# Attention and a gated MLP on one core: visits taken out of a pair's last step, differences, roundings and a weight conversion put elsewhere in their queues

## The chip, the cores and the metric

The kernel runs on one core of one Trainium2 chip. The metric is the time on the device in microseconds, the median of several runs. The engines of the core are called TensorE (PE; PEld for its weight loads), VectorE (DVE), ScalarE (ACT), GpSimd (POOL) and SyncE (SP), which here issues the transfers.

## What is computed

Eight batches of eight heads attend over 576 positions with 64 values a head. Four heads see a window of 32 positions, four see every fourth of the last 128. The result, 4608 tokens by 512, goes through a layer of 2048 with the gate h * erf(softplus(h)). The two weight matrices come as float64.

```python
scores = scale * np.matmul(q, k.transpose(0, 1, 3, 2))
...
masks = np.stack([mask_plain if h < H // 2 else mask_dil for h in range(H)], axis=0)
scores = np.where(masks[None, :, :, :], scores, -1000000000.0)
...
attn = attn / (np.sum(attn, axis=-1, keepdims=True) + 1e-09)
return np.matmul(attn, v).astype(np.float32)
...
h = x @ w_in
sp = np.maximum(h, 0.0) + np.log1p(np.exp(-np.abs(h)))
g = h * erf(sp)
return (g @ w_out).astype(np.float32)
```

## The kernel before

Every product of the MLP is made of three matmuls of rounded operands: high by high, high by low, low by high. A number is split into `hi`, its rounded value, and `lo`, the rounded remainder. `split` (L608) does that for a gate: a copy to `ghi` (L611; on VectorE, but on ScalarE for items of kind B) and a subtraction to `glo` (L612, VectorE).

**Attention** is cut into 72 units. A unit is scored in one visit (`scores`, L217, TensorE; `mask_max`, L228, eight masks for two units, VectorE), gets its exponents later (`exponents`, L238, ScalarE, with a table load ahead), is normalized (`normalize`, L249 and L250 on VectorE, L251 on GpSimd), and three visited units later it is turned (`transposes`, L256, TensorE, and the copy to `pT`, L260, VectorE) and multiplied with the values (`values`, L275, TensorE), and its rows are copied out (`rows`, L317, ScalarE). The first fourteen units are visited ahead of the MLP and seven in half steps 0 to 6, one each; later visits take two units at once. `PACE` and `visits` say where those stand: in 15 half steps from 9 to 39, and then in the periods 0 to 7 and 16 to 19.

**The MLP, first part.** Three chunks of 512 tokens are done in 24 steps of two half steps each, x = 0 to 47. A half step makes twelve products of the first matrix (L521, into the bank `h` or `tx`), takes the bank (L593), and twelve products of the second matrix (L636, into four accumulators `acc`) for the step two back, whose gate was computed in between: Softplus (L597), Erf (L600), product (L605), split. `weights` turns one more piece of the float64 weights into hi and lo (`prep_act`: L439 and L444, ScalarE; `prep_dve`: L453, L457 to L459, VectorE). At half step 11 (`SAVED`) the sums of chunk 0 are put aside: `save` copies the four accumulators (L650, two on VectorE, two on ScalarE) and stores them. The products of half step 12 that start the next sums need the accumulators empty.

**The second part** does the last six chunks in three pairs. A pair takes seven products instead of eight for four blocks (the scheme of Strassen in Winograd's form): the sums of weights are made by `build` in half steps 29 to 47 (L531, L540 to L543, L553, L557, stored to and read back from `ws`), the differences of tokens T1 to T4 by `big_less` (L716, VectorE), and each of B11, B21, B22, T1 to T4 is split by `big_hi` (L729, ScalarE) and `big_lo` (L733, VectorE). `FORE` and `AFT` list these jobs by half step and by (period, place in it).

A **period** (`period`, L837) is one step of this part. If it has a step d, it makes the seven products k = 0 to 6 (L768, six matmuls each, into `h` and `tx` in turn) and takes each from its bank on VectorE (`take_big`: L778, L776, L788). Between them stand four `quarter`s of six matmuls of the second matrix for the period's item (L636). Period i does the products of step d, Softplus for it (L801), Erf (L877) and the product (`multiply_big`, L805) for step d - 1, and the second matrix for the item i, whose first half is split a period earlier, its second at the period's start. Periods 0 to 7 are the first pair, 16 to 23 the second, 32 to 39 the third; periods 8 to 15 and so on have an item alone. In period 7 the products are grouped 3, 2, 2 and 0, so that the next Softplus starts early. The order of the products is A11 with B11, A12 with B21, S2 with T2, S3 with T3, A22 with T4, S1 with T1, S4 with B22.

All engines work strictly in the order in which the code is written, each in its own queue.

Of the kernel before, what the change touches and what calls it, by code (L numbers as in the profile page):

```python
# [41 lines left out]
NU = NIT * NBLK // PER  # L42
# [23 lines left out]
LAG = 3  # L66
# [6 lines left out]
SAVED = 2 * (HALF + 1) + 1  # L73
# [6 lines left out]
PART = 4  # L80
RIGHT = ("B11", "T3", "B21", "T2", "T1", "B22", "T4")
BUILD = 2 * SPC * 2 - 3
PACE = [9, 13, 15] + list(range(17, 40, 2))
BIG = {2 * SPC * k + d: SPC * k + d for k in range(DOUBLES) for d in range(SPC)}
ORDER = ("A11", "A12", "S2", "S3", "A22", "S1", "S4")

# [1 line left out]
def visits():  # L88


    at = {n - FIRST: [n] for n in range(FIRST, 2 * NBLK + LAG)}
    for x, n in zip(PACE, range(2 * NBLK + LAG, NU + LAG, 2)):
        at[x] = [n, n + 1]
    n, late = max(n for ns in at.values() for n in ns) + 1, {}
    for i in BIG:
        if n < NU + LAG:
            late[i] = [m for m in (n, n + 1) if m < NU + LAG]
            n += 2
    assert n >= NU + LAG
    return at, late  # L100
# [39 lines left out]
def attn_moe_kernel(ctx: ExitStack, tc: tile.TileContext, qk, v, masks, eye, w_in, w_out, out):  # L140
# [261 lines left out]
    def doubles(i):  # L402
        return io.tile([P, TOK, 2], I32, name=f"dbl{i}", bufs=1)
# [10 lines left out]
    def hold(on):  # L414
        held[0] = on
        while behind and not on:
            load, args = behind.pop(0)
            load(*args)
# [163 lines left out]
    def cell(i):  # L582
        return win[:, i * 2 * TOK:(i + 1) * 2 * TOK].rearrange("p (i n) -> p i n", i=2)
# [24 lines left out]
    def split(item, e, copy=None):  # L608
        ghi, glo = (work.tile([P, TOK], F32R, name=n) for n in ("ghi", "glo"))
        gs[item].append((ghi, glo))  # L610
        (copy or nc.vector.tensor_copy)(out=ghi, in_=e)  # L611
        nc.vector.tensor_tensor(out=glo, in0=e, in1=ghi.bitcast(F32), op=ALU.subtract)  # L612
# [28 lines left out]
    def copy_for(tt):  # L641
        return nc.scalar.copy if tt % 2 else nc.vector.tensor_copy

    def save():

        o = doubles(2).bitcast(F32).rearrange("p n w -> p (n w)")
        spare = small.tile([P, DM], F32, name="o", bufs=1)
        for tt in range(TOK // P):
            part = [o[:, 0:DM], o[:, DM:2 * DM], spare, pz[1]][tt]
            copy_for(tt)(out=part, in_=acc[tt])  # L650
            nc.sync.dma_start(out=partial[tt], in_=part)
# [7 lines left out]
    def store(c):  # L659
        last = c == NCH - 1  # L660
        for tt in range(TOK // P):
# [3 lines left out]
            else:  # L665
# [4 lines left out]
                else:  # L670
# [7 lines left out]
                    T3=(cell(6), cell(2 * len(RIGHT) + 1)), T1=xp[0:2], T4=xp[2:4]), {}  # L678
# [45 lines left out]
    def room_of(name):  # L724
        return lambda: raw[name]
# [5 lines left out]
    def big_lo(name):  # L731
        for p, r in zip(big[name], raw[name]):
# [3 lines left out]
    LESS = {n: (big_less, n, *FROM[n], room) for n, room in  # L736
            (("T3", room_w), ("T1", room_p), ("T2", room_w), ("T4", room_of("T2")))}
    HI, LO = ({n: (f, n) for n in RIGHT} for f in (big_hi, big_lo))

    FORE = {41: [(big_load, 0, ("B22",), room_w), (big_load, 0, ("B12", "B11", "B21"))],  # L740
            42: [LESS["T3"], HI["B11"]], 43: [LESS["T1"], HI["B21"]], 44: [LESS["T2"][:-1] + (room_of("B22"),)],
            45: [HI["T2"], LO["B11"]], 46: [LO["T2"]],
            47: [LESS["T4"], LO["B21"], (big_places,), (big_load, 0, ("B22",)), HI["T3"], HI["T4"], HI["T1"]]}
    AFT = {(0, 0): [LO["T3"]], (0, 1): [LO["T4"], HI["B22"]], (0, 2): [LO["T1"], LO["B22"]]}
    for k in range(1, DOUBLES):
        i = 2 * SPC * k
        first, then = (("B11", "B21"), ("B12", "B22")) if k == 1 else (("B12", "B22", "B11", "B21"), ())
        AFT.update({(i - 8, 0): [(big_load, k, first)], (i - 8, 3): [(big_load, k, then)],
                    (i - 6, 3): [LESS["T1"], LESS["T3"], HI["B11"], HI["B21"]],
# [67 lines left out]
    def split_item(item, j):  # L817
        e = ls[item] if item == NT - 2 else hs[item]
        split(item, e[:, j], nc.scalar.copy if isinstance(item, tuple) and item[0] == "B" else None)
# [17 lines left out]
    def period(i, late):  # L837
        d, item = BIG.get(i), ITEMS[i]
# [21 lines left out]
        def quarter():  # L860
            for _, args in zip(range(6), rest_):
                mm(args)

        for u in pending:
            exponents(u)
        split_item(item, 1)
        third(0)
        jobs(AFT.get((i, 0), ()))
        quarter()
# [4 lines left out]
        elif behind_ is not None:  # L874
            for kind_ in "AB":
                e = ls[kind_, behind_]
                nc.scalar.activation(out=e, in_=e, func=AF.Erf)  # L877
        jobs(AFT.get((i, 1), ()))
        quarter()
# [11 lines left out]
        if ahead is not None:  # L891
            split_item(ahead, 0)
        jobs(AFT.get((i, 2), ()))
        last_ = 6 in groups[2]
# [15 lines left out]
        if i + 3 < len(ITEMS) and isinstance(ITEMS[i + 3], tuple):  # L910
            load_g(ITEMS[i + 3])
        jobs(AFT.get((i, 3), ()))
        for n in ns:
# [10 lines left out]
    with tc.manual_schedule():  # L924
# [20 lines left out]
        def weights(x):  # L945
            if x not in pause:
                prep_act()
                prep_dve(keep=2 if SAVED - 4 < x <= SAVED else None)
# [3 lines left out]
        for x in range(2 * NT):  # L952
# [47 lines left out]
            if j == 1 and t < NT:  # L1000
                argument(t)
            if t >= 2:
                weights(x)
                mm2(t - 2, j)
                if x == SAVED:
                    save()
                    hold(False)
                    load_w(2)
                elif ends(t - 2):
                    if j == 1:  # L1010
                        store(STEPS[t - 2][0])
                    elif STEPS[t - 2][2] == 2:
                        fetch()
# [109 lines left out]
```

## Time and profile before

| | us |
|---|---|
| three runs | 905.57, 906.27, 907.35 |
| median | 906.27 |
| profiled execution, its own time | 906.74 |
| span of its trace, first to last instruction | 904.9 |
| TensorE busy | 874.4 |
| VectorE busy | 633.8 |
| ScalarE busy | 565.5 |
| GpSimd busy | 77.4 |

Busy time counts an engine's own instructions, not its waits and not the issuing of transfers. Matmuls overlap, and the profile draws each with a modelled end, so idle time on TensorE is read from the places where it says what TensorE waited for. A row of the timeline has the start, the length, the engine, the line, the operation and the tiles it writes and reads, and in brackets the idle time of the engine before it and what ended it.

### The profile page before, as it was taken

How to read it: one execution, taken by the hardware profiler on the slowest of the kernel's cores; microseconds unless marked ns; L12 is line 12 of the kernel's file. 1: busy time of each engine (PE TensorE's matmuls, PEld its weight loads, DVE VectorE, ACT ScalarE, POOL GpSimd, SP SyncE). 2: the span in 40 equal slices, each digit the busy share in tenths (PEclk: the TensorE clock that was granted, in tenths of full speed). 3: DMA queues.
4: the chain of work that ended last, by engine and by line, in shares of the span. 5: the costliest groups of instructions: out<-in, count | busy, mean ns of one | idle time of the engine just before them, and what ended most of it. 6: DMA issues, size and time to landing. Idle time of an engine off the chain costs nothing. (4 is left out here: it accounts for less than half of the span.)

```text
span 904.9 us, 20855 instructions
## 1 busy us (share of the span) xinstructions
PE 874.4 (97%) x8122; PEld 704.5 (78%) x8134; DVE 633.8 (70%) x1575; ACT 565.5 (62%) x1271; POOL 77.4 (9%) x97
## 2 busy tenths in 40 slices
PE   7799999999999999999999899899999999999998
PEld 3467878888888887788887688688888888888886
DVE  5888978987798888786776565576657647666622
ACT  6889978898788877566766552574544433535321
POOL 1212101111111100010010000000000000000000
PEclk9899999999999999999999999999999999999999
DMA  8874435464758886466665841474449225442341
GB/s 275 298 249 144 147 117 186 159 224 125 232 187 282 306 300 233 154 248 209 227 220 175 296 165 49 142 268 168 172 148 344 83 82 197 163 151 82 130 150 47
DMA packets 66915, 170.41 MB, mean 188 GB/s; under 512 B 7680, under 2 KB 14592, under 8 KB 63744
## 3 DMA queue, kind: packets, MB, share of 16 engines
q1 hardware_dynamic: 66528, 168.55, 54.1%
q8 instruction: 64, 1.05, 0.5%
q10 hardware_dynamic: 288, 0.52, 0.2%
q14 instruction: 35, 0.29, 0.1%
HBM read 122.91 MB, written 46.14 MB: 187 GB/s over the span
## 5 line engine op out<-in xcount | busy, mean ns | idle before, releaser
L636 PE MATMUL acc<-wout_hi,ghi 128*128 128x512 f32 x576 | 228.4, 397 | 5.7 <-DVE ghi L611 3.7
L636 PE MATMUL acc<-wout_lo,ghi 128*128 128x512 f32 x576 | 225.7, 392 | 0.0
L636 PE MATMUL acc<-wout_hi,glo 128*128 128x512 f32 x576 | 160.2, 392 | 0.0
L636 PEld LDWEIGHTS acc<-wout_hi,ghi 128*128 128x128 f32 x576 | 108.6, 189 | 28.3 <-DVE ghi L611 4.1
L636 PEld LDWEIGHTS acc<-wout_hi,glo 128*128 128x128 f32 x576 | 109.1, 189 | 23.3
L636 PEld LDWEIGHTS acc<-wout_lo,ghi 128*128 128x128 f32 x576 | 108.8, 189 | 21.9
L251 POOL TENSOR_TENSOR prob<-prob,rinv 128x256 f32<-128x256 f32 x72 | 70.5, 987 | 493.3 <-DVE ssum L249 269.8
L238 ACT ACTIVATE prob<-prob,nmax 128x64 f32<-128x64 f32 x288 | 96.4, 339 | 10.9 <-DVE nmax L228 10.7
L801 ACT ACT_TABLE_LOAD x24 | 30.8, 1283 | 97.4 <-DVE hc L776 49.8
L768 PE MATMUL tx<-win 128*128 128x512 f32 x288 | 74.9, 395 | 4.2 <-DVE hc L778 3.6
L228 DVE CUSTOM_DVE_ANT_0 prob<-sp,cst 128x64 f32<-128x64 f32 x288 | 45.3, 219 | 42.9 <-ACT rows L317 30.9
L768 PE MATMUL h<-win 128*128 128x512 f32 x288 | 75.2, 397 | 0.0
L768 PEld LDWEIGHTS tx<-win 128*128 128x128 f32 x288 | 53.5, 188 | 16.9 <-DVE hc L778 4.4
L768 PEld LDWEIGHTS h<-win 128*128 128x128 f32 x288 | 54.4, 191 | 12.3 <-DVE dbl L778 0.4
L612 DVE TENSOR_TENSOR glo<-hc,ghi 128x512 fp32r<-128x512 f32 x50 | 34.6, 692 | 38.3 <-PE acc L636 27.7
L238 ACT ACTIVATION_READ_ACCUMULATOR prob<-prob,nmax 128x1 f32 x288 | 54.9, 191 | 0.0
L612 DVE TENSOR_TENSOR glo<-dbl,ghi 128x512 fp32r<-128x512 f32 x48 | 33.2, 692 | 29.0 <-PE acc L636 17.5
L521 PE MATMUL h<-x,win 128*128 128x512 f32 x192 | 48.8, 396 | 0.0
L877 ACT ACTIVATE s<-s 128x1024 f32<-128x1024 f32 x48 | 48.2, 1052 | 0.3
L521 PE MATMUL tx<-x,win 128*128 128x512 f32 x192 | 48.0, 392 | 0.0
L801 ACT ACTIVATE s<-hc 128x1024 f32<-128x1024 f32 x24 | 25.5, 1061 | 35.4 <-DVE hc L776 22.9
L611 ACT CAST ghi<-hc 128x512 fp32r<-128x512 f32 x24 | 14.9, 622 | 49.1 <-PE acc L636 46.2
(146 smaller groups left out, 1518.0 us busy)
## 6 DMA issues: line engine op xcount, KB each, us to landing
win<-ws SPq DMA_DIRECT2D x24, 1024.0 KB, 5.0
v<-in_v_dram SPq DMA_DIRECT2D x72, 256.0 KB, 4.8
win<-ws SPq DMA_DIRECT2D x24, 768.0 KB, 5.1
qk<-in_qk_dram SPq DMA_DIRECT2D x48, 272.0 KB, 4.7
dbl<-in_w_in_dram SPq DMA_DIRECT2D x16, 512.0 KB, 4.4
dbl<-in_w_out_dram SPq DMA_DIRECT2D x16, 512.0 KB, 4.2
ws<-x SPq DMA_DIRECT2D x32, 256.0 KB, 3.6
qk<-in_qk_dram SPq DMA_DIRECT2D x24, 288.0 KB, 4.4
```

What stands on the lines that cost most here:

```text
L228: nc.vector.tensor_tensor_reduce(out=pr[:, g, :], in0=sps[h][:, u % 2, p, :], in1=mask[QUADS.index(kinds(u, p))], scale=-SCALE, scalar=HUG ...
L238: nc.scalar.activation(out=probs[u][:, j, :], in_=probs[u][:, j, :], func=AF.Exp, scale=-1.0, bias=nmax[:, j:j + 1], accum_out=sums[u][:, ...
L251: nc.gpsimd.tensor_tensor(probs[u], probs[u], rinv.broadcast_to([P, 2 * PARTS, KEYS]), op=ALU.mult)
L521: nc.tensor.matmul((h, bank)[j], win_at[:, ftp, j, cc // 2, w, cc % 2, :], x[cc], start=(k == 0 and i == 0), stop=(k == CC - 1 and i == 2))
L611: (copy or nc.vector.tensor_copy)(out=ghi, in_=e)
L612: nc.vector.tensor_tensor(out=glo, in0=e, in1=ghi.bitcast(F32), op=ALU.subtract)
L636: nc.tensor.matmul(args["out"], args["lhsT"], args["rhs"], start=args["start"], stop=args["stop"])
L768: nc.tensor.matmul(bank_, w[:, wi, c, :], x[c][:, xi, :], start=(c == 0 and n == 0), stop=(c == 1 and n == 2))
L801: nc.scalar.activation(out=ls[kind_, d], in_=hs[kind_, d], func=AF.Softplus)
L877: nc.scalar.activation(out=e, in_=e, func=AF.Erf)
```

## The change

Five edits in one.

1. `PACE` gets one more entry, half step 41, and `visits` gives no visit to the last step of a pair (`i + 1 in BIG`). So there is a visit at half step 41 and none in period 7. Every unit between them is visited two units earlier than before; the four visits from period 16 on stay.
2. In `FORE` the difference T4 and the remainder of B21 move from half step 47 to 46.
3. In `AFT` the remainder of T1 moves from (0, 2) to (0, 1), ahead of the product and the split that stand between the two places.
4. In `period` the split of the item's second half comes ahead of the exponents.
5. At half step 11 alone, `weights` comes behind the copies of `save`, no longer ahead of the products.

```diff
-PACE = [9, 13, 15] + list(range(17, 40, 2))
+PACE = [9, 13, 15] + list(range(17, 42, 2))
...
-        if n < NU + LAG:
+        if n < NU + LAG and i + 1 in BIG:
...
-            45: [HI["T2"], LO["B11"]], 46: [LO["T2"]],
-            47: [LESS["T4"], LO["B21"], (big_places,), (big_load, 0, ("B22",)), HI["T3"], HI["T4"], HI["T1"]]}
-    AFT = {(0, 0): [LO["T3"]], (0, 1): [LO["T4"], HI["B22"]], (0, 2): [LO["T1"], LO["B22"]]}
+            45: [HI["T2"], LO["B11"]], 46: [LO["T2"], LESS["T4"], LO["B21"]],
+            47: [(big_places,), (big_load, 0, ("B22",)), HI["T3"], HI["T4"], HI["T1"]]}
+    AFT = {(0, 0): [LO["T3"]], (0, 1): [LO["T4"], LO["T1"], HI["B22"]], (0, 2): [LO["B22"]]}
...
+        split_item(item, 1)
         for u in pending:
             exponents(u)
-        split_item(item, 1)
...
             if t >= 2:
-                weights(x)
+                if x != SAVED:
+                    weights(x)
                 mm2(t - 2, j)
                 if x == SAVED:
                     save()
+                    weights(x)
                     hold(False)
```

ScalarE's queue around the end of period 7 and in period 8, before: after the last Softplus (L801) come the visit's row copies (L317), the table load and the exponents (L238), and then Erf (L877) for the step of period 7.

```order
L801 ACTIVATE s<-hc 128x1024 x2
L317 COPY rows<-sp_90 128x112
L317 COPY rows<-sp_90 128x16
L317 COPY rows<-sp_91 128x128
L317 COPY rows<-sp_90 128x128
L317 COPY rows<-sp_91 128x128
L238 ACT_TABLE_LOAD
L238 ACTIVATE prob,ssum<-prob,nmax 128x64 x8
L877 ACT_TABLE_LOAD
L877 ACTIVATE s<-s 128x1024 x2
```

The same place now:

```order
L801 ACT_TABLE_LOAD
L801 ACTIVATE s<-hc 128x1024 x2
L877 ACT_TABLE_LOAD
L877 ACTIVATE s<-s 128x1024 x2
L611 CAST ghi<-dbl_6631 128x512
```

The rows of the visit are gone from between Softplus and Erf.

ScalarE's queue at the start of period 17, as a piece of the difference; `ghi` (L611) is the rounding of the item's second half.

```order
 L317 COPY rows<-sp_91 128x128
-L238 ACT_TABLE_LOAD
-L238 ACTIVATE prob,ssum<-prob,nmax 128x64 x8
 L611 CAST ghi<-hc 128x512
+L238 ACT_TABLE_LOAD
+L238 ACTIVATE prob,ssum<-prob,nmax 128x64 x8
 L877 ACT_TABLE_LOAD
```

The rounding now stands ahead of the table load and the exponents.

VectorE's queue in period 0, before, from taking the fourth product (`tx`) to taking the fifth (`h`) and the sixth (`tx`): `x_99` and `x_100` are the remainder of T4, `x_97` and `x_98` that of T1, `dbl_4955` and `plain` that of B22.

```order
L776 TENSOR_TENSOR dbl_4978<-tx,dbl_4978 128x512
L733 TENSOR_TENSOR x_99<-w,x_99 128x512
L733 TENSOR_TENSOR x_100<-w,x_100 128x512
L605 TENSOR_TENSOR hc<-hc,s 128x1024
L611 CAST ghi<-hc 128x512
L612 TENSOR_TENSOR glo<-hc,ghi 128x512
L733 TENSOR_TENSOR x_97<-pT_88,x_97 128x512
L733 TENSOR_TENSOR x_98<-o,x_98 128x512
L733 TENSOR_TENSOR dbl_4955<-dbl_4955 128x512
L733 TENSOR_TENSOR plain<-plain 128x512
L776 TENSOR_TENSOR dbl_4977<-h,dbl_4978 128x512
L788 TENSOR_TENSOR dbl_4978<-tx,dbl_4978 128x1024
```

The same place now:

```order
L776 TENSOR_TENSOR dbl_5088<-tx,dbl_5088 128x512
L733 TENSOR_TENSOR x_99<-w,x_99 128x512
L733 TENSOR_TENSOR x_100<-w,x_100 128x512
L733 TENSOR_TENSOR x_97<-pT_88,x_97 128x512
L733 TENSOR_TENSOR x_98<-o,x_98 128x512
L605 TENSOR_TENSOR hc<-hc,s 128x1024
L611 CAST ghi<-hc 128x512
L612 TENSOR_TENSOR glo<-hc,ghi 128x512
L733 TENSOR_TENSOR dbl_5065<-dbl_5065 128x512
L733 TENSOR_TENSOR plain<-plain 128x512
L776 TENSOR_TENSOR dbl_5087<-h,dbl_5088 128x512
L788 TENSOR_TENSOR dbl_5088<-tx,dbl_5088 128x1024
```

The remainder of T1 stands ahead of the product and the split of the item; between the fourth product and the fifth stand the same nine instructions as before.

## Prediction before the run

> **What bounds the kernel now.** I read the page first, for the busiest engine, and then the table of waits for TensorE (engine and line, what it waited for, us in total, times, longest).
>
> ```profile
> PE 874.4 (97%) x8122; PEld 704.5 (78%) x8134; DVE 633.8 (70%) x1575; ACT 565.5 (62%) x1271; POOL 77.4 (9%) x97
> ...
> PE acc L636 <- DVE ghi L611: 3.7, 1, 3.7
> PE tx L768 <- DVE hc L778: 3.6, 2, 2.6
> ...
> PE tx L768 <- DVE x L733: 2.0, 1, 2.0
> PE acc L636 <- DVE dbl L650: 2.0, 1, 2.0
> ...
> PE tx L768 <- DVE win L733: 0.6, 1, 0.6
> PE sp L275 <- DVE pT L260: 0.6, 1, 0.6
> ```
>
> TensorE is busy 97% of the span, and the change takes no matmul away. So only TensorE's idle time can be won, and time in which it runs slowly. The waits listed here make 12.5 us, seven in number, each on VectorE; they stand at half step 11, in period 0, in periods 7 and 8, and in period 17. (The second wait on L778, 0.9 us, is at the start of period 7, and the change leaves it.)
>
> The second view is the table of stretches, cut along the steps in which the granted clock changes (length, busy time of PE, PEld, DVE, ACT and POOL, then the clock, DMA share, GB/s).
>
> ```profile
> 121.71:125.12 3.41, 1.44 (x7) 1.18 (x7) 3.38 (x6) 3.36 (x5) 0.00 (x0) 1.00 0.18 69
> 125.12:128.54 3.42, 3.42 (x10) 2.63 (x9) 0.77 (x2) 1.11 (x1) 0.00 (x0) 0.50 1.04 352
> ...
> 364.06:367.47 3.41, 1.67 (x7) 1.05 (x6) 3.20 (x5) 0.00 (x0) 0.00 (x0) 1.00 0.70 276
> 367.47:370.88 3.41, 3.14 (x16) 2.61 (x17) 3.31 (x6) 0.76 (x1) 0.00 (x0) 1.00 0.00 0
> 507.42:510.83 3.41, 0.49 (x2) 0.44 (x3) 2.09 (x3) 2.01 (x3) 0.00 (x0) 1.00 0.81 287
> 510.83:514.24 3.41, 3.41 (x10) 2.64 (x9) 2.42 (x4) 0.47 (x1) 0.00 (x0) 0.50 0.38 142
> ...
> 572.27:575.68 3.41, 1.05 (x5) 0.88 (x6) 1.98 (x3) 3.38 (x8) 0.00 (x0) 1.00 0.34 125
> 575.68:579.10 3.42, 3.42 (x10) 2.64 (x9) 0.69 (x1) 0.88 (x1) 0.00 (x0) 0.50 0.02 5
> ```
>
> Three of the waits are paid twice. A stretch of 3.41 us in which TensorE was busy 1.44, 0.49 or 1.05 us is followed by one at half clock, which does 1.71 us less work. After 1.67 us busy the clock stayed whole. So in this trace the limit lies between 1.44 and 1.67 us busy, and the half clock is part of the price of the three long waits.
>
> The chain of waits gives the pace of matmuls that wait for nothing (start, us, what):
>
> ```profile
> 661.96 1.36 PE h L768 x6
> ```
>
> That is 0.227 us each. The profile draws a lone matmul 0.39 us long, so an idle stretch it shows starts 0.17 us after the next matmul could have started. Each wait therefore costs 0.17 us more than its listed length.
>
> **Half step 11: one weight conversion behind the copies.** Rows of the timeline (start, us, engine, line, operation, tiles; in brackets the idle time before and its releaser):
>
> ```profile
> 120.60 0.68 DVE L453 TENSOR_TENSOR win<-w,win 128x512 fp32r<-128x512 f32 x1
> ...
> 122.99 0.68 DVE L650 COPY dbl<-acc 128x512 f32<-128x512 f32 x1
> ...
> 123.73 0.50 PE L636 MATMUL acc<-wout_hi,ghi 128*128 128x512 f32 x1 [1.97 <-DVE dbl L650]
> ...
> 131.15 0.69 DVE L593 COPY hc<-tx 128x512 f32<-128x512 f32 x1 [5.22 <-PE tx L521]
> ```
>
> Now the copy starts where L453 started, at 120.60, and ends at 121.28; TensorE may go on 0.06 later, as it did before, at 121.34. It is ready at 123.73 - 1.97 - 0.17 = 121.59. The wait goes with 0.25 us to spare, and with it its half clock: 1.97 + 0.17 + 1.71 = **3.85 us**. What moves back is the conversion, by two copies, 1.36 us, on VectorE, and by two on ScalarE. Behind it stand the copy of h and the roundings for the next products; VectorE then sat idle 5.22 us before 131.15, and this covers 1.36 us and TensorE's earlier arrival of 3.85. Cost nothing; without that cover 1.36.
>
> **Period 0: differences and roundings moved ahead.**
>
> ```profile
> 352.30 0.69 DVE L593 COPY hc<-tx 128x512 f32<-128x512 f32 x1 [3.12 <-PE tx L521]
> ...
> 355.23 1.28 DVE L716 TENSOR_TENSOR w<-win,w 128x512 f32<-128x512 f32 x2
> 356.44 1.28 DVE L733 TENSOR_TENSOR win<-win 128x512 fp32r<-128x512 f32 x2
> ...
> 362.73 0.69 DVE L776 TENSOR_TENSOR dbl<-tx,dbl 128x512 f32<-128x512 f32 x1 [0.67 <-PE tx L768]
> ...
> 369.40 0.69 DVE L776 TENSOR_TENSOR dbl<-h,dbl 128x512 f32<-128x512 f32 x1
> ...
> 361.17 1.52 PE L768 MATMUL tx<-win 128*128 128x512 f32 x6
> ...
> 370.83 0.86 PE L768 MATMUL h<-dbl,win 128*128 128x512 f32 x3
> ```
>
> The four instructions of T4 and B21 (2.56 us) move from period 0 into half step 46, in front of the row at 352.30, where VectorE idled 3.12 us. B21's remainder is then there before the second product of period 0 asks for it: 0.60 + 0.17 = 0.77 us saved.
>
> The remainder of T1 moves in front of L605, L611 and L612, so the sixth product gets it in time, and its wait of 2.01 + 0.17 = 2.18 us goes. But VectorE still has the same work between taking the fourth product (362.73) and the fifth (369.40): 6.67 us from start to start. The seventh product writes into the bank that the fifth leaves, so it waits for that second row. Counted from the start of the fourth product: VectorE takes it 362.73 - 361.17 = 1.56 later, and the bank is free 1.56 + 6.67 + 0.69 + 0.05 = 8.97 later. TensorE arrives 370.83 - 361.17 - 2.18 = 7.48 later. **A new wait of 1.49 us stands at the seventh product**, and of 2.18 only 0.69 is kept. Sum: 0.77 + 0.69 = **1.46 us**. A wait of 1.49 leaves 1.9 of 3.41 us busy, above the 1.67 after which the clock stayed whole.
>
> **Periods 7 and 8: no visit in the last step.**
>
> ```profile
> 498.45 1.06 ACT L801 ACTIVATE s<-hc 128x1024 f32<-128x1024 f32 x1 [3.61 <-DVE hc L776]
> ...
> 506.15 1.28 ACT L877 ACT_TABLE_LOAD   x1
> 507.44 2.00 ACT L877 ACTIVATE s<-s 128x1024 f32<-128x1024 f32 x2
> ...
> 505.58 1.07 PE L636 MATMUL acc<-wout_hi,glo 128*128 128x512 f32 x4
> 510.34 0.50 PE L636 MATMUL acc<-wout_hi,ghi 128*128 128x512 f32 x1 [3.69 <-DVE ghi L611]
> ```
>
> Between the last Softplus (ends 499.51) and the table load of Erf (506.15) ScalarE copied rows and made the visit's sixteen exponents. Without the visit the load follows at once, at about 499.53. From that load to the matmul it released took 510.34 - 506.15 = 4.19 us, so ghi is there at 503.72. TensorE without waits was ready at 510.34 - 3.69 - 0.17 = 506.48; without the visit, which costs it 2.44 us (below), and without its wait for pT (0.59 + 0.17 = 0.76), at 503.28. **A wait of 0.44 us is left.** Saved: 0.76 + 3.86 + 1.71 - 0.44 = **5.89 us**.
>
> On what a change of table costs, a page speaks against this sum. The Trainium skill, "ScalarE: Activation LUTs", section "What ACT_TABLE_LOAD costs", puts every switch at about 2.66 us, 1.38 of it a drain beside the load. The trace has the Erf begin 1.29 us after its load began and shows no drain. By the page the load could not follow the Softplus so closely, the wait left would be an estimated 1.8 us and the saving 4.5.
>
> **Period 17: the split ahead of the exponents.**
>
> ```profile
> 568.68 1.28 ACT L238 ACT_TABLE_LOAD   x1 [0.17 <-DVE nmax L228]
> ...
> 572.64 0.60 ACT L611 CAST ghi<-hc 128x512 fp32r<-128x512 f32 x1
> ...
> 574.62 2.05 PE L768 MATMUL tx<-win 128*128 128x512 f32 x6 [2.65 <-DVE hc L778]
> ```
>
> The rounding on ScalarE (572.64) stood behind the exponents; behind it, on VectorE, stood the remainder and the copy that frees tx. From the rounding to the matmul took 1.98 us. Ahead of the exponents it starts by 568.68 and TensorE is released by 570.7, or by 571.3 if VectorE's masks come first. TensorE is ready at 574.62 - 2.82 = 571.80. So 2.65 + 0.17 + 1.71 = **4.53 us**. Rounding and exponents only change places, so the Erf behind them keeps its place; TensorE, 4.53 us earlier, needs its result two quarters later.
>
> **Half step 41: the visit that comes in.**
>
> ```profile
> 303.27:311.15 7.88, 7.88 (x158) 6.43 (x156) 6.76 (x14) 6.16 (x12) 2.02 (x2) 1.00 0.61 234
> 333.06:338.50 5.44, 5.44 (x25) 4.50 (x24) 5.34 (x9) 5.17 (x8) 0.00 (x0) 1.00 0.64 234
> ...
> 320.27 0.16 DVE L249 TENSOR_SCALAR ssum<-ssum 128x4 f32<-128x4 f32 x1
> ...
> 371.33 0.75 DVE L260 COPY pT<-sp 128x256 f32<-128x256 f32 x2
> ...
> L228 DVE CUSTOM_DVE_ANT_0 prob<-sp,cst 128x64 f32<-128x64 f32 x288 | 45.3, 219 | 42.9 <-ACT rows L317 30.9
> ```
>
> A half step with a visit lasts 7.88 us, one without 5.44: a visit is 2.44 us of TensorE. It leaves period 7 and enters half step 41, so it costs nothing by itself. It brings VectorE 8 masks (45.3 / 288 x 8 = 1.26 us), two copies (0.75) and four small ones (some 0.65): 2.66 us against TensorE's 2.44. ScalarE gets the rows, a table load and sixteen exponent instructions; SyncE four loads and a store, in front of the stores of the sums. VectorE was already busy 5.34 of 5.44 us in a step like 44, and half step 46 gets its 2.56 on top. So it ends half step 47 without idle time and about an us behind its old place, still in time for period 0's first roundings. Between no loss and 2 us (a rounding that is late once) I allow **0.5 us** of loss, nearer to nothing, because no half step with visit and sums from 31 to 39 shows a wait.
>
> **The sum.** 3.85 + 1.46 + 5.89 + 4.53 - 0.50 = 15.2 us. The profiled execution took 906.74 us (span 904.9 and 1.8 around it), 0.47 above the median of the three runs, 906.27. I take 906.27 - 15.2 = **891.1 us**. The runs lie within 905.57 to 907.35; 0.2%, 1.8 us, is about what a measurement of this kernel can tell from no change.
>
> **Rivals.** (1) *VectorE falls behind at half step 47*, and the new wait at the seventh product passes about 1.9 us, so that a half clock follows: 1.71 plus 0.5 to 2 us of waiting, 893.3 to 894.8. For it: the filled 3.12 us and the 5.34 of 5.44. Against: VectorE catches up at the fourth product, where it waits for TensorE (the 0.67 at 362.73). Chance 0.17.
>
> (2) *The half clock stays without the waits.* Then the three times 1.71 are not won: 891.1 + 5.1 = 896.2. For it: nothing but that three cases are few; against: each follows a stretch with little work. Chance 0.04. The Trainium skill, "TensorE: Matmul & The Clock Gate", sections "What's actually happening" and "HAM oscillation", has the clock fall back only after a whole idle window of some 3.4 us; by that rule none of these waits would have caused it. The stretches above, 1.05 and 1.44 us busy, disagree with the rule.
>
> (3) *Period 17 keeps its wait*, because the masks and not the rounding hold VectorE: 4.53 lost, 895.6. Against: the row at 568.68 has the first of them done by 568.5, and eight take 1.26 us. Chance 0.03.
>
> (4) *Slower: VectorE becomes the bound from half step 42 to 46.* Each of the five steps would have to wait over 2 us, so that a half clock follows each: 5 x (2.0 + 1.71) = 18.6 us, 18.6 - 15.2 = 3.4 above the old time, 909.7. It decides once VectorE is late by 10 us in five steps; the added work is 5.2, half of it met by TensorE's 2.44. Chance 0.02.
>
> **The numbers.** My case, 0.74, gives 888.7 (no wait at the seventh product, none at period 9, no loss at 41: 2.4 us better) to 893.3. With rival 1 the range is 888.7 to 894.8 and leaves out rivals 2 to 4 and the tails. Faster by over 0.2%: all but rival 4 and a remainder, 0.97; same 0.01; slower 0.02.
>
> **What would show it.** Right: no wait of TensorE on L650 near 121.6; no half clock after the warm-up; in period 0 one wait near 1.5 us, on the release of h by L776; near the start of period 9 one of about 0.4 on ghi; none at period 17; the 0.9 us of period 7 still there. Wrong: a half clock after half step 41 or the seventh product (rival 1), waits of acc on ghi between 322 and 357 (rival 4), a half clock without a wait before it (rival 2).

## The result, and the profile after

| | us |
|---|---|
| changed kernel, median of five runs | 892.89 (891.79 to 893.75) |
| the kernel before, median of five runs beside them | 906.27 (905.57 to 908.06) |
| ratio | 0.9847, 95% interval 0.9831 to 0.9863 |
| profiled execution of the changed kernel, its own time | 892.89 |
| span of its trace | 890.9 |

The changed kernel is 1.5% faster; 891.1 was forecast, with a range of 888.7 to 894.8. The profile below is read at the places that the prediction named. First the page's line of busy times and what is left in the table of waits for TensorE (us in total, times, longest).

```profile
PE 871.2 (98%) x8134; PEld 700.1 (79%) x8134; DVE 633.6 (71%) x1575; ACT 564.5 (63%) x1271; POOL 81.3 (9%) x97
```

```profile
PE h L768 <- DVE dbl L776: 1.5, 1, 1.5
...
PE tx L768 <- DVE hc L778: 0.8, 1, 0.8
PE acc L636 <- DVE ghi L611: 0.4, 1, 0.4
```

VectorE and ScalarE do what they did before; the waits went, and the half clocks behind them. The rows left out are waits in the warm-up, here the first 73 us. The 0.8 is the one in period 7 that the change leaves alone, the other two are the waits that the prediction left over, and no half clock falls behind the warm-up: the granted clock is 0.5 at 11.29 and at 42.01, for 3.41 us each, and never after that.

**Half step 11.** VectorE's rows of the timeline, then TensorE's.

```profile
121.32 0.69 DVE L612 TENSOR_TENSOR glo<-s,ghi 128x512 fp32r<-128x512 f32 x1
121.93 0.68 DVE L650 COPY dbl<-acc 128x512 f32<-128x512 f32 x1
...
123.12 0.68 DVE L453 TENSOR_TENSOR win<-w,win 128x512 fp32r<-128x512 f32 x1
...
128.57 0.69 DVE L593 COPY hc<-tx 128x512 f32<-128x512 f32 x1 [1.31 <-PE tx L521]
```

```profile
122.92 0.39 PE L636 MATMUL acc<-wout_hi,ghi 128*128 128x512 f32 x1
```

The copy ends at 122.61 and the matmul starts at 122.92 with no idle time in brackets: 0.31 apart, or 0.25 to spare when the 0.06 of the release is taken off, as the prediction had it. The cover behind it shrank from 5.22 to 1.31 us of idle time, and it held.

**Period 0.** VectorE takes the products with idle time before the second, the third (0.83, not shown) and the fourth; the one wait left is TensorE's, at the seventh product.

```profile
357.79 0.69 DVE L776 TENSOR_TENSOR dbl<-tx,dbl 128x512 f32<-128x512 f32 x1 [0.55 <-PE tx L768]
...
361.87 0.69 DVE L776 TENSOR_TENSOR dbl<-tx,dbl 128x512 f32<-128x512 f32 x1 [0.67 <-PE tx L768]
...
368.55 0.68 DVE L776 TENSOR_TENSOR dbl<-h,dbl 128x512 f32<-128x512 f32 x1
```

```profile
369.38 0.94 PE L768 MATMUL h<-dbl,win 128*128 128x512 f32 x3 [1.53 <-DVE dbl L776]
```

From the fourth product's taking to the fifth's it is 368.55 - 361.87 = 6.68 us (6.67 before), and the wait is listed with 1.53. The forecast of 1.49 counted from where TensorE was ready, which adds the 0.17: so counted the wait is 1.70. Of the 0.21 between them, 0.10 is the release (the matmul starts 0.15 after the copy's end at 369.23, where 0.05 was taken), the rest is TensorE's earlier arrival.

**Periods 7 and 8.** ScalarE goes from the last Softplus to the table load of Erf without a visit between them; TensorE waits 0.43 us as listed (0.44 forecast, counted from where it is ready; so counted it is 0.60).

```profile
496.70 1.06 ACT L801 ACTIVATE s<-hc 128x1024 f32<-128x1024 f32 x1 [3.83 <-DVE hc L776]
497.78 1.28 ACT L877 ACT_TABLE_LOAD   x1
499.07 2.01 ACT L877 ACTIVATE s<-s 128x1024 f32<-128x1024 f32 x2
```

```profile
501.98 0.50 PE L636 MATMUL acc<-wout_hi,ghi 128*128 128x512 f32 x1 [0.43 <-DVE ghi L611]
```

From table load to matmul it is 4.20 us (4.19 before). The load starts 0.02 us after the Softplus ends and Erf 1.29 after the load: no drain.

**Half step 41 and the five after it,** as stretches: the step with the visit, the next, and the last ahead of period 0 (PE, PEld, DVE, ACT, POOL busy; clock; DMA).

```profile
314.20:322.08 7.88, 7.88 (x158) 6.43 (x156) 6.24 (x12) 5.61 (x9) 1.74 (x2) 1.00 0.94 305
322.08:327.52 5.44, 5.44 (x30) 4.50 (x25) 5.16 (x24) 5.32 (x20) 0.00 (x0) 1.00 0.98 332
...
349.28:354.87 5.59, 5.59 (x27) 4.62 (x25) 5.52 (x10) 2.78 (x4) 0.00 (x0) 1.00 0.40 153
```

The visit costs 7.88 - 5.44 = 2.44 us of TensorE, and only the last half step is longer than 5.44, by 0.15.

**Period 17.** The rounding (L611) stands ahead of the table load, remainder and copy (L612, L778) behind the masks, and the matmul that waited 2.65 us starts with no wait.

```profile
558.99 0.66 ACT L611 CAST ghi<-hc 128x512 fp32r<-128x512 f32 x1
559.67 1.28 ACT L238 ACT_TABLE_LOAD   x1
```

```profile
560.16 0.69 DVE L612 TENSOR_TENSOR glo<-hc,ghi 128x512 fp32r<-128x512 f32 x1
560.76 0.69 DVE L778 COPY hc<-tx 128x512 f32<-128x512 f32 x1
```

```profile
562.44 0.39 PE L768 MATMUL tx<-win 128*128 128x512 f32 x1
```

**Where the time went.** Both traces are cut at the same matmuls, the first of half steps 0, 14, 41 and of periods 0, 1, 16 and 18:

| from, to | before | after | won | forecast |
|---|---|---|---|---|
| half step 0 to 14 | 87.11 | 83.23 | 3.88 | 3.85 |
| half step 41 to period 0 | 38.08 | 40.67 | -2.59: visit -2.44, rest -0.15 | rest -0.50 |
| period 0 to 1 | 20.70 | 19.28 | 1.42 | 1.46 |
| period 1 to 16 | 174.66 | 166.66 | 8.00; less the visit's 2.44, 5.56 | 5.89 |
| period 16 to 18 | 39.53 | 34.95 | 4.58 | 4.53 |

That makes 15.3 us, where 15.2 was forecast. The times of the two profiled executions, 906.74 and 892.89, differ by 13.9, since half step 0 itself starts at 48.95 in the one and at 50.30 in the other. That start belongs to the execution, not to the kernel: the code ahead of it is the same in all kernels here, and over their fourteen profiles it lies between 48.25 and 52.91.

Between periods 1 and 16 0.33 us are missing. Period 12 shows a cost there that the prediction had no term for. These are SyncE's and ScalarE's rows of after:

```profile
510.53 0.34 SPq L674 DMA_DIRECT2D out_dram<-o  x1
511.00 1.35 SPq L674 DMA_DIRECT2D out_dram<-w  x3
512.41 1.46 SPq L814 DMA_DIRECT2D hc<-g  x2
```

```profile
517.86 0.62 ACT L611 CAST ghi<-hc 128x512 fp32r<-128x512 f32 x1 [4.54 <-DMA hc<-g]
```

The gates of the pair's second chunk come back from memory (L814) behind the loads of tokens and the stores of the sums. Rows of before for the same load and the same rounding:

```profile
519.87 1.29 SPq L814 DMA_DIRECT2D hc<-g  x2
```

```profile
524.99 0.62 ACT L611 CAST ghi<-hc 128x512 fp32r<-128x512 f32 x1 [2.10 <-PE acc L636]
```

TensorE reaches the end of these periods 550.18 - 540.81 = 9.4 us earlier, SyncE issues the load only 519.87 - 512.41 = 7.5 earlier. So ScalarE's rounding, which waited for TensorE, now waits 4.54 us for the transfer. In this execution TensorE loses an estimated half a microsecond by it; in a second one of the same kernel the wait is drawn:

```profile
518.83 0.50 PE L636 MATMUL acc<-wout_hi,ghi 128*128 128x512 f32 x1 [0.76 <-ACT ghi L611]
```

What it costs differs from execution to execution: in the five traces that have the changed kernel's code from period 1 to 16 (after, after_again, t4_early, probe_4, probe_8, all explained below) that stretch lasts 166.10 to 167.50 us, where 166.33 was forecast.

### The profile page after: what moved, and what is told of

Read it like the earlier page. It is cut to its first block, busy times and chain, and to the rows that moved or that the text cites. A ratio compares the mean times of both kernels' runs of the same rounds, so it can differ in the third digit from the quotient of the medians.

```text
span 890.9 us, 20870 instructions
## 1 busy us (share of the span) xinstructions
PE 871.2 (98%) x8134; PEld 700.1 (79%) x8134; DVE 633.6 (71%) x1575; ACT 564.5 (63%) x1271; POOL 81.3 (9%) x97
## 3 DMA queue, kind: packets, MB, share of 16 engines
q8 instruction: 64, 1.05, 0.5%
## 4 chain that ended last, share of the span: by engine, by line
PE 91%; DVE 5%; DMA 1%; ACT 1%; issue 1%; POOL 1%; SPq 0%; DVEq 0%; POOLq 0%; ACTq 0%
PE acc L636 43%; PE h L768 13%; PE tx L768 13%; PE h L521 7%; PE tx L521 7%; PE sp L275 3%; PE sp L217 3%; PE sp L256 1%; PE h L357 1%; DMA qk<-in_qk_dram 1%; DMA v<-in_v_dram 1%; DVE w L458 0%; DVE w L459 0%; DVE prob L228 0%; DVE win L453 0%
## 5 line engine op out<-in xcount | busy, mean ns | idle before, releaser
L251 POOL TENSOR_TENSOR prob<-prob,rinv 128x256 f32<-128x256 f32 x72 | 72.7, 1016 | 477.0 <-DVE ssum L249 239.9
L238 ACT ACTIVATE prob<-prob,nmax 128x64 f32<-128x64 f32 x288 | 96.3, 338 | 10.5 <-DVE nmax L228 10.3
L612 DVE TENSOR_TENSOR glo<-hc,ghi 128x512 fp32r<-128x512 f32 x50 | 34.5, 692 | 33.4 <-PE acc L636 22.6
L238 ACT ACTIVATION_READ_ACCUMULATOR prob<-prob,nmax 128x1 f32 x288 | 54.7, 190 | 0.0
L612 DVE TENSOR_TENSOR glo<-dbl,ghi 128x512 fp32r<-128x512 f32 x48 | 33.4, 696 | 28.3 <-PE acc L636 15.6
L877 ACT ACTIVATE s<-s 128x1024 f32<-128x1024 f32 x48 | 48.2, 1052 | 0.3
L801 ACT ACTIVATE s<-hc 128x1024 f32<-128x1024 f32 x24 | 25.5, 1061 | 34.9 <-DVE hc L776 22.8
L611 ACT CAST ghi<-hc 128x512 fp32r<-128x512 f32 x24 | 14.9, 623 | 50.0 <-PE acc L636 41.9
```

Source lines behind the costliest of these rows:

```text
L238: nc.scalar.activation(out=probs[u][:, j, :], in_=probs[u][:, j, :], func=AF.Exp, scale=-1.0, bias=nmax[:, j:j + 1], accum_out=sums[u][:, ...
L251: nc.gpsimd.tensor_tensor(probs[u], probs[u], rinv.broadcast_to([P, 2 * PARTS, KEYS]), op=ALU.mult)
L801: nc.scalar.activation(out=ls[kind_, d], in_=hs[kind_, d], func=AF.Softplus)
```

## The experiments

### The parts one by one

Four kernels, each the kernel before with one part of the change: the copies first (edit 5), the visits (edit 1), the split first (edit 4), the differences and roundings (edits 2 and 3).

```diff
 copies_only
-                weights(x)
+                if x != SAVED:
+                    weights(x)
 visits_only
-PACE = [9, 13, 15] + list(range(17, 40, 2))
+PACE = [9, 13, 15] + list(range(17, 42, 2))
-        if n < NU + LAG:
+        if n < NU + LAG and i + 1 in BIG:
 split_only
+        split_item(item, 1)
         for u in pending:
             exponents(u)
-        split_item(item, 1)
 jobs_only
-46: [LO["T2"]], 47: [LESS["T4"], LO["B21"], ...
+46: [LO["T2"], LESS["T4"], LO["B21"]], 47: [...
-(0, 1): [LO["T4"], HI["B22"]], (0, 2): [LO["T1"], LO["B22"]]
+(0, 1): [LO["T4"], LO["T1"], HI["B22"]], (0, 2): [LO["B22"]]
```

Expected of the copies alone:

> The kernel before with one edit alone: at half step 11 the weight conversion stands behind the copies of the sums. Theory (a wait is paid with the half clock that follows it, and both go with it): the wait of 1.97 us on L650 and the half clock after it are gone, 1.97 + 0.17 + 1.71 = 3.85 us faster than before; half clock after half step 12 nowhere; the waits of periods 0, 8 and 17 and the two half clocks behind them as before. Rival (the half clock belongs to the place, not to the wait): the stretch after half step 11 keeps its half clock, 2.1 us faster.

Expected of the visits alone:

> The kernel before with one edit alone: a visit at half step 41, none in period 7. Theory: the waits on pT and on ghi around period 8 and the half clock behind them go, a wait of 0.4 us on ghi stays, small waits for the returning gates show in period 12: 5.0 to 5.9 us faster than before. Period 17 keeps its 2.65 us wait and its half clock, half step 11 too; period 0 keeps its two waits. Rival (the added visit crowds VectorE in half steps 42 to 47, and it is this that makes the seventh product of period 0 wait): a wait of over 0.5 us on L776 at the seventh product shows here too, and only 4 us are won.

Expected of the split alone:

> The kernel before with one edit alone: in a period the split of the item's second half stands ahead of the exponents. Theory: it matters in period 17 alone, where the rounding is ScalarE's: the wait of 2.65 us and its half clock go, 4.5 us faster than before; period 8 keeps its 3.69 us wait, since there the exponents still stand ahead of Erf. Rival (half clock not tied to the wait): 2.8 us faster. Rival (VectorE's masks hold period 17): no gain over 1 us.

Expected of the differences and roundings alone:

> The kernel before with two edits alone: T4 and the remainder of B21 in half step 46, the remainder of T1 ahead of the product and the split in period 0. Theory (the queue of VectorE between taking the fourth and the fifth product is as long as before, so the wait moves on to the seventh product): the waits of 0.60 and 2.01 us go, one of 1.5 us stands before the seventh product, 1.5 us faster than before. Rival (that new wait comes from the visit at half step 41, which is not in here): no wait at the seventh product, 2.9 us faster.

Measured, against 29 runs of the kernel before on the same chip (median 906.88):

| kernel | median us | ratio, 95% interval | mean gain us | forecast for the part |
|---|---|---|---|---|
| copies_only | 904.05 (12 runs) | 0.9967, 0.9952 to 0.9982 | 2.8 | 3.85 |
| visits_only | 900.10 (6 runs) | 0.9930, 0.9908 to 0.9951 | 6.9 | 5.89 - 0.50 = 5.39 |
| split_only | 903.91 (12 runs) | 0.9974, 0.9958 to 0.9991 | 2.9 | 4.53 |
| jobs_only | 904.81 (12 runs) | 0.9978, 0.9964 to 0.9991 | 2.3 | 1.46 |

(The mean gain is against 906.71, the mean of the 47 runs of the kernel before that stand beside the experiments.) Each part removes its own waits and no other; the gains add up to 14.9, and the whole change gains 14.0 by the means (10 runs at 892.73). The parts do not interact beyond the spread. The wait at the seventh product comes with the differences and roundings alone, without the visit at half step 41:

```profile
369.35 0.94 PE L768 MATMUL h<-dbl,win 128*128 128x512 f32 x3 [1.53 <-DVE dbl L776]
```

So it is not VectorE crowded by the visit (rival 1) but the order of the work between the fourth and the fifth product. The split alone gains less than its forecast of 4.53; its interval reaches to 3.8 us. Its wait is gone in the trace, where periods 16 and 17 take 34.95 us. With the wait and the half clock behind it they take 39.53 (before), with the wait alone 37.94, 37.94 and 37.92 (copies_only, jobs_only, visits_only, which have no half clock there). So the wait is worth 3.0 us and both 4.58; the mean gain of 2.9 is the wait without the half clock. The next section looks at that half clock.

### Half clock: not behind every wait

The same four waits stand in several of these traces, and the half clock behind them is not always there:

| wait, us | before | copies_only | visits_only | split_only | jobs_only |
|---|---|---|---|---|---|
| half step 11, 2.0 | yes | (gone) | yes | no | yes |
| period 0, 2.0 | no | no | no | no | (gone) |
| period 8, 3.7 | yes | yes | (0.4) | yes | yes |
| period 17, 2.65 | yes | no | no | (gone) | no |

The stretches at half clock stand on a grid: in the trace of before they start at 32.96, 125.12, 510.83 and 575.68, which are 27, 113 and 19 times 3.413 us apart. So each trace can be cut along its own grid (us of the stretch, busy time of PE first, the clock behind POOL's). The split alone around half step 11, then the visits alone around period 17, and jobs_only around both:

```profile
118.84:122.26 3.42, 2.22 (x10) 1.50 (x8) 3.32 (x6) 2.20 (x4) 0.13 (x1) 1.00 0.01 5
122.26:125.67 3.41, 2.64 (x12) 2.19 (x13) 2.94 (x6) 3.36 (x5) 0.00 (x0) 1.00 0.56 216
```

```profile
564.94:568.35 3.41, 1.73 (x8) 1.11 (x6) 0.38 (x1) 3.39 (x18) 0.00 (x0) 1.00 0.84 220
568.35:571.76 3.41, 2.44 (x11) 2.00 (x12) 2.29 (x4) 2.90 (x3) 0.00 (x0) 1.00 0.09 31
```

```profile
121.30:124.71 3.41, 1.44 (x7) 1.00 (x6) 3.34 (x7) 3.38 (x5) 0.00 (x0) 1.00 0.11 42
124.71:128.12 3.41, 3.41 (x10) 2.62 (x9) 0.99 (x2) 1.54 (x2) 0.00 (x0) 0.50 0.97 334
568.45:571.86 3.41, 2.11 (x10) 1.41 (x8) 0.00 (x0) 3.38 (x19) 0.00 (x0) 1.00 0.91 226
571.86:575.27 3.41, 2.06 (x9) 1.69 (x10) 2.33 (x4) 3.28 (x3) 0.00 (x0) 1.00 0.19 70
```

A wait that lies across a line of the grid is shared out (2.65 us into 1.30 and 1.35 in the last two rows), no stretch falls below the limit, and the clock stays whole. The limit of the prediction, between 1.44 and 1.67 us busy, holds in all of these. In all fourteen traces it holds for every stretch at full clock that starts after 70 us. The nearest two stand side by side in jobs_only, around the wait of period 8; the clock stays whole after the first and is half after the second:

```profile
503.59:507.00 3.41, 1.66 (x8) 1.05 (x6) 0.55 (x4) 3.38 (x10) 1.23 (x2) 1.00 0.91 272
507.00:510.42 3.42, 1.47 (x6) 1.24 (x7) 3.07 (x4) 1.05 (x2) 0.00 (x0) 1.00 0.72 252
```

In the first 70 us, where TensorE also has the many small matmuls of attention, it does not hold. In visits_only a stretch busy 1.73 us is followed by a half clock:

```profile
59.77:63.18 3.41, 1.73 (x69) 1.54 (x70) 1.89 (x11) 3.40 (x13) 0.61 (x1) 1.00 0.98 358
63.18:66.59 3.41, 3.41 (x10) 2.67 (x9) 3.34 (x10) 3.38 (x6) 0.00 (x0) 0.50 0.80 264
```

Why the limit is another there is not shown.

Two probes test it on purpose: in the changed kernel, four or eight subtractions on an unused tile stand ahead of the copies of half step 11 and hold them up.

```diff
                 if x == SAVED:
+                    for _ in range(4):  # or 8
+                        nc.vector.tensor_tensor(out=plain[:, 0:256], in0=plain[:, 0:256], in1=plain[:, 0:256], op=ALU.subtract)
                     save()
```

> The changed kernel with four subtractions of 128x256 (on an unused tile) on VectorE ahead of the copies of half step 11; they change no result. They put back a wait of TensorE there, of a length short of the one that the change removed. Theory (a wait is paid a second time by the half clock only if it leaves one of the stretches of 3.41 us, which stand on a grid of their own, with less than about 1.5 us of work; a wait of this length cannot): a wait of 1.1 to 1.6 us at half step 11, no half clock behind it, the granted clock of the runs as in the changed kernel (about two stretches at half clock in a run), 894.2 us. Rival (any wait over a microsecond is paid twice): half clock behind it, 895.9.

> The same with eight subtractions. Theory: a wait of 2.5 to 3.4 us at half step 11; most of the executions, 2 in 3 or more, show a half clock behind it and one stretch more at half clock than the changed kernel (about 2.8 in the mean), 897.3 us. Rival 1 (the half clock needs a stretch with no work at all, which a wait of this length cannot leave): no half clock, the clock of the runs as in the changed kernel, 896.0. Rival 2 (every wait over 1.9 us is paid twice, whatever the grid): one stretch more in each run, 897.7; the mean of the clock alone tells rival 2 from the theory badly, the profile tells rival 1 from both.

Measured: 893.80 us (4 runs, ratio 0.9856, 0.9836 to 0.9875) and 897.24 (5 runs, 0.9899, 0.9880 to 0.9917). In the traces the waits are 1.29 and 3.13 us. Their runs have 2.9 and 3.4 stretches at half clock on the average, where about 2 and 2.8 were expected. With four there is no half clock behind the wait; with eight there is one:

```profile
122.92:126.33 3.41, 2.12 (x10) 1.43 (x9) 3.31 (x8) 3.37 (x4) 0.00 (x0) 1.00 0.10 41
...
126.33:129.74 3.41, 3.41 (x17) 2.79 (x16) 3.31 (x6) 2.01 (x2) 0.00 (x0) 1.00 0.83 294
```

```profile
124.98:128.39 3.41, 0.73 (x4) 0.27 (x2) 3.18 (x8) 3.37 (x4) 0.00 (x0) 1.00 0.00 0
128.39:131.80 3.41, 2.95 (x7) 2.38 (x8) 3.34 (x7) 1.78 (x2) 0.00 (x0) 0.50 0.66 254
```

The stretch ahead of the half clock was not idle: 0.73 of its 3.41 us were work. So the rival that asks for a stretch with no work falls, as does the one that has any wait over a microsecond paid twice. The rival that has every wait over 1.9 us paid twice falls by the table above, not by the probe.

The granted clock of each run gives the time at half clock, twice (1 - clock) times the span. Over those 47 runs of the kernel before that is 4.8 stretches of 3.41 us a run, over 35 runs of the seven kernels without its three long waits (the changed one, run in two rounds of measurement, probe_4 and the five below) 2.5. By this estimate the three waits together cost 2.3 stretches a run, give or take 0.5: 2.3 x 1.71 = 3.9 us, where one execution showed 3 x 1.71 = 5.1. The ten runs of the changed kernel alone have 2.0, which makes 2.8, give or take 1, and does not exclude 3. All of them count those of the first 70 us too, 1 to 5 in the fourteen profiles, so the count is a rough measure. The runs of split_only have 4.9 and those of copies_only 4.7, no fewer than the 4.8 of before: on the average, taking out one of the two shorter waits saved its length and hardly a half clock.

### What is left: the changed kernel with further edits

Beside one another ran the changed kernel again, T4's remainder a place earlier in period 0, the last step's products grouped otherwise, and these two with the loads of the returning gates written ahead of the stores.

```diff
 t4_early
-(0, 0): [LO["T3"]], (0, 1): [LO["T4"], LO["T1"], HI["B22"]]
+(0, 0): [LO["T3"], LO["T4"]], (0, 1): [LO["T1"], HI["B22"]]
 groups
-            groups = [(0, 1, 2), (3, 4), (5, 6), ()]
+            groups = [(0, 1), (2, 3, 4), (5, 6), ()]
 together: both, and
+        if i + 3 < len(ITEMS) and isinstance(ITEMS[i + 3], tuple):
+            load_g(ITEMS[i + 3])
         if done(item) is not None:
             store(done(item))
...
-        if i + 3 < len(ITEMS) and isinstance(ITEMS[i + 3], tuple):
-            load_g(ITEMS[i + 3])
```

> The changed kernel unchanged, a second profile. Theory (the half clock follows any stretch of a fixed grid of 3.41 us in which TensorE was busy under about 1.6 us; the warm-up falls on that grid differently in each execution): from half step 0 to the end TensorE takes the same time as in the first profile within 0.3 us, while half step 0 starts anywhere between 48.2 and 52.2 us, and the clock of the runs spreads. Rival (the change itself made the warm-up 1.3 us longer): half step 0 starts at 50.3 us again.

> The changed kernel with the remainder of T4 moved from (0, 1) to (0, 0) of period 0, into the 0.55, 0.83 and 0.67 us for which VectorE waits there. Theory (the wait of the seventh product is the length of VectorE's queue between taking the fourth and the fifth product): the queue is 1.29 us shorter, the wait of 1.53 us shrinks to about 0.2, 1.3 us faster than the changed kernel, about 14.7 us faster than before. Rival (the seventh product waits for the remainder of B22 or something else): its wait stays over 1 us.

> The changed kernel with the last step's products grouped 2, 3, 2, 0 where they were 3, 2, 2, 0. Theory (the wait of 0.79 us at the third product of period 7 stands there because no quarter lies between it and the second): it goes, 0.9 us faster than the changed kernel; the wait on ghi before period 9 stays 0.4 us, since the fifth product ends where it did. Rival (it moves on, because VectorE's queue is what is late): the wait on ghi before period 9 grows by as much, no gain.

> The changed kernel with three edits: the remainder of T4 in (0, 0), the last step's products grouped 2, 3, 2, 0, and the loads of the returning gates issued ahead of the stores of finished sums. Theory (each wait is paid by itself): 1.3 + 0.9 + 0.5 = 2.7 us faster than the changed kernel, 16 to 17 us faster than before. Rival (VectorE or the transfers are the bound behind these waits): under 1.5 us faster than the changed kernel.

Measured, against nine runs of the kernel before (median 906.51):

| kernel | median us | ratio, 95% interval |
|---|---|---|
| after_again | 892.91 (5 runs) | 0.9848, 0.9832 to 0.9864 |
| t4_early | 891.64 (4 runs) | 0.9837, 0.9819 to 0.9855 |
| groups | 891.30 (4 runs) | 0.9834, 0.9817 to 0.9850 |
| together | 891.80 (4 runs) | 0.9848, 0.9827 to 0.9869 |

In its second profile the changed kernel starts half step 0 at 49.75, where it was 50.30, and takes 0.84 us longer from there to the end. At most 0.3 was expected. The 0.84 lie between periods 1 and 16 (167.50 against 166.66), with the wait of 0.76 us shown above.

With T4's remainder taken out from between the fourth and the fifth product, the wait at the seventh shrinks by 1.10 us, to 0.43 where about 0.2 was expected:

```profile
369.13 0.94 PE L768 MATMUL h<-dbl,win 128*128 128x512 f32 x3 [0.43 <-DVE dbl L776]
```

The other grouping removes the 0.79 of period 7 and leaves the 0.44 before period 9 as it is. All three edits together should have been the fastest, 2.7 us under the changed kernel, and are 1.1 under it by the medians; a wait that was not there stands in the periods of the returning gates. TensorE's row, and VectorE's:

```profile
516.96 0.73 PE L636 MATMUL acc<-wout_hi,glo 128*128 128x512 f32 x2 [2.22 <-DVE glo L612]
```

```profile
514.41 0.69 DVE L716 TENSOR_TENSOR o<-win 128x512 f32<-128x512 f32 x1 [5.27 <-DMA out_dram<-w]
...
516.22 0.69 DVE L612 TENSOR_TENSOR glo<-dbl,ghi 128x512 fp32r<-128x512 f32 x1
```

VectorE's differences for the second pair wait 5.27 us until the stores of the sums have left their tiles (1.46 us in the changed kernel), and the remainder (L612) that TensorE needs is queued behind them. My theory for this edit was wrong: a load moved ahead of a store delays the store, and someone waits for that too. Two more kernels take it apart: the first two edits without the third, and the third alone.

> The changed kernel with the two edits that each took one of its waits: the remainder of T4 one place earlier in period 0, and the last step's products grouped 2, 3, 2 and 0; the loads of the returning gates stay where the change left them. Theory (the loads moved ahead of the stores cost the 2.22 us wait that the version with all three edits showed, since the rest of it was these two): no wait over 1 us in the periods of returning gates; waits of 0.43 at the seventh product and 0.44 before period 9, none in period 7; from the first product of period 0 to that of period 1 18.1 us, from the last product of period 7 to the first of period 8 about 48.5; 890.9 us, 1.2 and 0.8 below the changed kernel. Rival (the two edits together bring the wait, the order of the loads does not matter): a wait of about 2.2 us on the low remainder near 515 here as well, and about 893.

> The changed kernel with the loads of the returning gates written ahead of the stores of the sums, nothing else. Theory (this order costs time, since the stores then land later and VectorE's differences for the next pair wait for them): a wait of some 2 us on a low remainder near 517, and 1 to 2 us above the changed kernel, 894 to 895. Rival (the order of the loads costs nothing and wins the 0.5 us of small waits near 518): no such wait, 892.4.

Measured, against nine runs of the kernel before (median 907.07): two_waits 889.54 (5 runs, 889.32 to 890.01, ratio 0.9810, 0.9796 to 0.9824), load_first 894.33 (4 runs, 0.9862, 0.9846 to 0.9878). What is left in the table of waits of two_waits, and load_first's new wait:

```profile
PE acc L636 <- DVE ghi L611: 0.4, 1, 0.4
PE h L768 <- DVE dbl L776: 0.4, 1, 0.4
```

```profile
519.93 1.20 PE L636 MATMUL acc<-wout_hi,glo 128*128 128x512 f32 x4 [0.89 <-DVE glo L612]
```

The order of the loads brings the wait, the other two edits don't. By itself it is 0.89 us, less than the 2 expected; with TensorE 2 us earlier, in the version with all three, it is 2.22. What it costs by itself is not shown. From the last product of period 7 to the first of period 16 load_first takes 49.51 us, between the 48.95 and the 49.79 of the changed kernel's two profiles; with all three edits it is 50.89, against 48.51 in two_waits. The runs of load_first have 1.2 stretches at half clock more than those of the changed kernel, which is 2.0 us and more than the 1.4 between the medians. **two_waits beats both kernels:** 3.3 us under the changed one by the medians, where 2.0 was expected; where the rest comes from is not shown.

## Why the prediction came out right

- **Half step 11** (3.85): right, with the 0.25 us to spare that was worked out, and the cover held. The half clock in it was there in three traces of four that have this wait.
- **Period 0** (1.46): right, 1.42, and the new wait where it was put, 1.70 for 1.49 (1.53 as listed). The near match is partly luck: counted from the period's start, the third product gained 0.91 where 0.77 was forecast, the seventh 0.59 more where it was 0.69, and 0.08 was lost behind it. The step that carried it was to count VectorE's work between two takings, instead of only striking out the wait that the edit removes.
- **Periods 7 and 8** (5.89): the mechanism right, the wait left 0.60 for 0.44 (0.43 as listed). The term was 0.33 too large in this execution, most likely because the transfers of period 12 don't come earlier at TensorE's pace; no row of that queue was priced, and what it costs differs from one execution to the next. The page "ScalarE: Activation LUTs" of the Trainium skill, section "What ACT_TABLE_LOAD costs", with its drain, would have left an estimated 1.8 us; the trace disagrees with it, with Erf 1.29 us after the load's start.
- **Half step 41** (loss of 0.50): 0.15. VectorE took the bank of half step 47 3.22 us after that half step's start (352.50 - 349.28), where it had been 2.92 (352.30 - 349.38), so 0.3 later and not an us; it was busy 5.16 of 5.44 us in the step behind the visit and 5.52 of 5.59 in the last, and TensorE lost no more than the 0.15.
- **Period 17** (4.53): right in the profile, 4.58, with the masks ahead of the remainder as in the slower of the two cases that were worked out.
- **The sum:** its time came out 1.8 us too low. The term that was mis-sized is the half clock, "paid twice" for three waits: it was read off one execution in which all three happened to be. In the traces it stands behind 3 of 4 waits at half step 11, 4 of 4 in period 8 and 1 of 4 in period 17, on the average two stretches instead of three; the granted clocks make it 2.3, 1.2 us less, with the uncertainty given above. The rest of the 1.8 is within what the start of half step 0 does from run to run. The profile's 15.3 for 15.2 owes something to luck too: the trace of before happened to hold all three half clocks.
- **Rivals.** 1 (VectorE late at half step 47, half clock at the seventh product): no, the wait is there without the visit, and with it stays at 1.5. 2 (half clock without waits): no, none is left behind the warm-up in the two profiles of the changed kernel. Its page, "TensorE: Matmul & The Clock Gate" of the Trainium skill, is right in "What's actually happening" that the window of 3413 ns runs freely, as the grid shows; that it has to be idle throughout the traces contradict, with 0.73 and 1.44 us busy ahead of a half clock. Only the wait of 3.69 us is long enough to leave such a stretch with no work, and in split_only it does (0.00 us busy from 504.55 to 507.96). 3 and 4: no wait in period 17, none in half steps 42 to 46.

What stays open: how many half clocks in the first 70 us an execution gets and how late its half step 0 starts, and how much of the 14.0 us of the means is half clock. No run here was made to tell that.

## What to carry to other kernels

When an edit takes a wait away, follow the engine that was waited for to its next deadline: the work between two takings stays, and what is left of the wait moves there. When TensorE gains some us, each queue that feeds it must gain them too; here the transfers were the ones that didn't. A price that one trace shows for a wait (here the half clock) is a draw: look at the other runs' clocks before it is counted in full.

## What the runs showed of the hardware

- After the first 70 us, the half clock follows a stretch of a fixed grid of 3.413 us in which TensorE, at full clock, was busy 1.47 us or less by the profile (0.00, 0.49, 0.70, 0.73, 1.05, 1.44 three times and 1.47 in these traces) and not one with 1.66 or more. In the first 70 us it also followed one busy 1.73 us. So the same wait is paid twice or not by where it falls: with a limit of 1.75 to 1.94 us idle, a wait w that may start anywhere does it in (3.41 + w - 2 x limit) / 3.41 of the cases, an estimated 0.4 to 0.6 for 2.0 us, 0.6 to 0.8 for 2.65 and 0.9 or more for 3.7; seen in 3 of 8, 1 of 4 and 4 of 4. The 3 of 8 are 3 of 4 at half step 11 and 0 of 4 in period 0.
- Half clock can hold on. In copies_only the wait of 3.69 us ran on into the stretch at half clock, which was then busy 2.44 of 3.41 us, and the next stretch stayed at half too:

```profile
505.25:508.66 3.41, 0.70 (x4) 0.23 (x2) 1.19 (x3) 3.38 (x5) 0.94 (x2) 1.00 0.95 334
508.66:512.07 3.41, 2.44 (x6) 1.96 (x7) 3.10 (x6) 0.08 (x1) 0.00 (x0) 0.50 0.48 165
512.07:515.49 3.42, 3.42 (x10) 2.64 (x9) 0.85 (x2) 0.62 (x1) 0.00 (x0) 0.50 0.98 285
```

But in probe_8 a stretch at half clock that was busy 2.95 us was followed by a whole one, and in split_only one busy 3.29 us (507.96 to 511.37). In the first 70 us stretches at half clock busy 2.90 us (before, at 32.96) and 3.31 us (probe_8, at 43.06) stayed at half clock. What ends a half clock is open.
